# Softmax sums in the middle of a head's turn, and the last head's sums on all partitions

## The chip, the cores and the metric

The kernel runs on one core of a Trainium2 chip. Its time is device microseconds (us) of one launch; the number compared is the median of several runs. The engines are TensorE (PE, matrix products into the eight PSUM banks; its weight loads are listed as PEld), VectorE (DVE), ScalarE (ACT), GpSimd (POOL) and SyncE (SP), whose queue issues nearly all DMA transfers. Each engine works through its own instructions in order and waits on semaphores for the others.

## The reference

Four layers, A, B, A, B, on one sequence of 2048 positions and 640 channels. A is a filter in the frequency domain, and the change doesn't touch it. B is attention in segments of 32 positions with 8 memory positions ahead of each; the memory of a segment is the output of the segment before at those 8 places:

```python
mem = mem0
for s in range(n_seg):                       # 64 segments
    xs = x[:, s * seg_len:(s + 1) * seg_len, :].copy()
    h = jnp.concatenate([mem, xs], axis=1)   # 40 rows
    q, k, v = (einsum('btd,dhe->bhte', h, W) for W in (Wq, Wk, Wv))    # 32 heads of 128
    scores = einsum('bhqe,bhke->bhqk', q, k) * scale
    scores = jnp.where(mask[None, None], scores, -1000000000.0)
    p = _softmax(scores, axis=-1)
    o = einsum('bhqk,bhke->bhqe', p, v)
    o = einsum('bhte,hed->btd', o, Wo)
    mem = o[:, :M, :].copy()
    outs.append(o[:, M:, :])
...
x = x + _A_ref(_layernorm(x), A_w_r, A_w_i)
x = x + _B_ref(_layernorm(x), ...)           # layer 1 below
x = x + _A_ref(_layernorm(x), A_w_r, A_w_i)
x = x + _B_ref(_layernorm(x), ...)           # layer 2 below
```

## The kernel before

**The fast pass.** The kernel guesses the memories, so that all segments can be computed at once, and checks the guess at the end of each B layer; if it fails, or a sum is out of range, a slow exact pass runs (it doesn't run on this input). "Layer 1" and "layer 2" mean the two B layers. Everything here is in `_b_fast_pass`, once per layer. It works on all 64 segments of one head at a time, transposed: the head's 128 features lie on the partitions, the queries (2119 columns: 64 x 32 positions, one memory column a segment and a few more) along the free axis. They form five groups: four of 495 columns (15 segments) and one of 139.

**A head's turn.** The loop over h runs 34 turns for 32 heads, as a pipeline of three stages. Turn h does, in this order:
- for head h, the projections: five key runs (`k_run`, PE L840 into `psk`, copied by DVE L899), five query runs (`q_run`, `psq`, copied by ACT L884 to L892) and value tiles for a pair of heads (`v_tiles`, PE L906 into `psv`, ACT L908), five runs in even turns and four in odd ones. They share three PSUM banks, the pool `pj`.
- for head h-1, nine score parts (`score_part`): PE L916 into `pss` (two banks), ACT takes Exp (L919), DVE multiplies by the mask (L920), which gives P, not normalised.
- for head h-2, five value groups (`value_group`): PE L959 into `pso` (two banks), then DVE multiplies by the inverse softmax sums (L963 for the positions, L965 for the memory column), which frees the bank.

`merge` deals the score parts and value groups evenly between the projection runs, so the score parts stand beside the keys and queries, the value groups beside the last query run and the value tiles. The order on PE, ACT and DVE is that of the code; SP's and POOL's instructions are placed by the framework's scheduler.

**The sums.** At the end of turn h, `sums` adds up P of head h-1 on PE (L934, with 32 columns of ones, one group to 32 partitions of bank `psl`, the fifth group into a free corner of the last score bank), and ACT copies the sums to SBUF (L938 to L940). Behind the first score part of the next turn, ACT takes Ln and Exp(-x) of them (L943, L946), which gives the inverses R. They lie on five rows and are needed on all 128 partitions: SP writes them to DRAM (`Rd`, L948, L949) and a third DMA, L950, broadcasts them into Rb (two buffers). POOL adds R and the sums to two running sums for a range check (`accR` L951, `accS` L952).

**Stores.** At the end of a turn, the head's output goes to DRAM (L972, 512 KB). After every fourth head the first 512 positions of these four heads are loaded back (L975) for the output projection, and that load waits for the store.

**The end of a layer.** In turns 32 and 33 there are no projections left. There `begin` starts three pieces of the output projection, each of 28 matmuls (L1112, into `psx`) over the first 28 heads; the rest of the output projection follows later. The last head's sums go the same way as all others, through DRAM. Behind it stands the memory check (`_b_mem_check`, PE L617), whose range test reads `accR` and `accS` on DVE (L641 to L644).

## Time and profile before

| | |
|---|---|
| median of 3 runs (lowest, highest) | 1707.96 us (1707.82, 1707.96) |
| span of the profiled execution | 1706.2 us |
| layer 1: turns of the loop with all three stages / end of the heads | about 180 to 690 us / 701.6 to 732.1 us |
| layer 2: the same | about 1009 to 1531 us / 1537.0 to 1567.3 us |
| PE busy in layer 2's loop (1009 to 1537 us) | 514.0 of 528.0 us |
| POOL busy in it | 92.0 us |

All rows below come from one profiled execution. A row of the timeline reads: start in us, duration in us, engine, line of the kernel, operation, output <- inputs, shape; in square brackets the time that the engine stood idle before it and what ended that wait. SPq marks the moment when SP issues a DMA; the transfer itself lands later. A row with "x5" holds five like instructions in a row. A row of waits reads: engine, its tile and line, <- what it waited for, then total us, number of waits, the longest. A row of windows reads: stretch, its length, then the busy us of PE, PEld, DVE, ACT and POOL (number of instructions in brackets), mean granted PE clock as a share of the full one, share of DMA time, GB/s.

### The profile page before, as it was taken

The page shows a single profiled execution, that of the slowest core. Times are in us where ns is not written, and L with a number is a line of the kernel's source. Part 1 is how long each engine was busy: PE and PEld are TensorE (multiplying, and loading weights), DVE is VectorE, ACT ScalarE, POOL GpSimd, SP SyncE. Part 2 cuts the span into 40 slices and gives each one's busy share as a digit, 9 for nine tenths or more (in the row PEclk, how much of TensorE's full clock was granted, in tenths as well). Part 3 has the DMA queues.
Part 4 walks back from the last instruction along what each step waited for, and adds up shares of the span by engine and source line. Part 5 has one row for each costly group of instructions (what it writes and reads, how often), then busy time and mean ns, then how long its engine had stood idle before and what let it go on. Part 6 is the DMA issues. An engine that isn't in the chain of part 4 may idle for free. (4 is left out here: it accounts for less than half of the span.)

```text
span 1706.2 us, 36149 instructions
## 1 busy us (share of the span) xinstructions
PE 1570.4 (92%) x14202; PEld 1087.9 (64%) x14203; DVE 906.5 (53%) x2308; ACT 844.0 (49%) x2514; POOL 268.7 (16%) x192
## 2 busy tenths in 40 slices
PE   4887999999999999799987889999999999997998
PEld 2565666666666666577755666666666666665776
DVE  5973465565656555543357725556655665654111
ACT  5363566666666666411114636656666666662000
POOL 0520111121212121200015001112111121211000
PEclk9997999999999999999999989999999999999999
DMA  4562134434343434643301803334343344347232
GB/s 150 170 237 80 62 136 138 139 113 145 128 138 125 141 133 140 218 155 93 94 13 55 283 2 121 125 116 152 133 140 125 135 140 138 115 159 229 66 113 67
DMA packets 168180, 220.23 MB, mean 129 GB/s; under 512 B 7416, under 2 KB 141888, under 8 KB 159808
## 3 DMA queue, kind: packets, MB, share of 16 engines
q1 hardware_dynamic: 167392, 215.53, 37.8%
q8 instruction: 113, 1.85, 0.5%
q0 software_dynamic: 608, 2.30, 0.4%
q14 instruction: 67, 0.55, 0.1%
HBM read 172.69 MB, written 45.11 MB: 128 GB/s over the span
## 5 line engine op out<-in xcount | busy, mean ns | idle before, releaser
L920 DVE TENSOR_TENSOR bB_S<-bB_S,maskf 128x269 bf16<-128x269 bf16 (+5 forms) x576 | 273.2, 475 | 229.4 <-ACT bB_S L919 226.3
L840 PEld LDWEIGHTS <-bB_S 128*128 128x128 bf16 x3180 | 262.7, 97 | 206.6 <-issue 20.8
L1112 PE MATMUL psx<-Wo_sb,bB_S 128*128 128x320 bf16 x2048 | 289.9, 301 | 1.1 <-DVE bB_S L963 1.1
L919 ACT ACTIVATE bB_S<-pss 128x269 bf16<-128x269 f32 (+5 forms) x576 | 224.9, 392 | 112.5 <-PE pss L916 65.3
L963 DVE TENSOR_TENSOR bB_S<-pso,bB_S 128x480 bf16<-128x480 f32 (+1 forms) x320 | 186.0, 582 | 159.0 <-PE pso L959 89.5
L908 ACT CAST bB_S<-psv 128x512 bf16<-128x512 f32 (+1 forms) x288 | 161.8, 562 | 185.7 <-PE psv L906 182.0
L1112 PEld LDWEIGHTS <-bB_S 128*128 128x128 bf16 x2048 | 198.6, 98 | 77.0 <-DVE bB_S L963 1.4
L952 POOL TENSOR_TENSOR bB_S<-bB_S,bB_S 128x634 f32<-128x634 f32 x64 | 98.6, 1540 | 933.1 <-ACT bB_S L940 933.1
L899 DVE CAST bB_S<-psk 128x495 bf16<-128x495 f32 (+3 forms) x320 | 188.9, 591 | 91.5 <-PE psk L840 91.2
L884 ACT ACTIVATE bB_S<-psq 128x480 bf16<-128x480 f32 x300 | 154.2, 514 | 76.2 <-PE psq L840 76.2
L916 PEld LDWEIGHTS <-bB_S 128*128 128x128 bf16 x1216 | 111.3, 98 | 103.2 <-issue 2.3
L906 PE MATMUL psv<-bB_S,B2hT_S 128*128 128x256 bf16 x1360 | 172.3, 274 | 0.2 <-DVE bB_S L899 0.2
L906 PE MATMUL psv<-bB_S,B1hT_S 128*128 128x256 bf16 x1360 | 171.0, 272 | 0.2 <-DVE bB_S L899 0.2
L840 PE MATMUL psk<-B1hT_S,bB_S 128*128 128x495 bf16 (+3 forms) x800 | 162.9, 343 | 1.2 <-DVE B1hT_S L1197 1.2
L840 PE MATMUL psk<-B2hT_S,bB_S 128*128 128x495 bf16 (+3 forms) x800 | 162.9, 343 | 1.2 <-DVE B2hT_S L1197 1.2
L916 PE MATMUL pss<-bB_S 128*128 128x132 bf16 (+8 forms) x1216 | 159.9, 216 | 1.8 <-ACT bB_S L919 1.7
L840 PE MATMUL psq<-B2hT_S,bB_S 128*128 128x495 bf16 (+5 forms) x780 | 154.5, 335 | 7.2 <-DVE bB_S L899 7.2
L840 PE MATMUL psq<-B1hT_S,bB_S 128*128 128x495 bf16 (+5 forms) x780 | 154.5, 335 | 6.7 <-DVE bB_S L899 6.7
L959 PE MATMUL pso<-bB_S,bB_S 128*128 128x132 bf16 (+8 forms) x1216 | 121.2, 218 | 30.0 <-DVE oTmf L965 29.8
L906 PEld LDWEIGHTS <-B2hT_S 128*128 128x128 bf16 x1360 | 127.2, 98 | 13.1 <-issue 0.3
L906 PEld LDWEIGHTS <-B1hT_S 128*128 128x128 bf16 x1360 | 126.5, 98 | 12.6 <-issue 0.3
L959 PEld LDWEIGHTS <-bB_S 128*128 128x128 bf16 x1216 | 92.9, 99 | 44.0 <-DVE oTmf L965 36.9
(216 smaller groups left out, 1553.4 us busy)
## 6 DMA issues: line engine op xcount, KB each, us to landing
bB_S<-Rd SPq DMA_DIRECT2D x64, 1059.5 KB
oTx_d<-bB_S SPq DMA_DIRECT2D x60, 512.0 KB
bB_S<-oTx_d SPq DMA_DIRECT2D x56, 512.0 KB
bB_S<-in_B_Wq_dram SPq DMA_DIRECT2D x32, 320.0 KB
bB_S<-in_B_Wk_dram SPq DMA_DIRECT2D x32, 320.0 KB
bB_S<-in_B_Wv_dram SPq DMA_DIRECT2D x32, 320.0 KB
bB_S<-oTx_d SPq DMA_DIRECT2D x14, 384.0 KB
Wo_sb<-in_B_Wo_dram SPq DMA_DIRECT2D x4, 1280.0 KB
```

Source lines behind the costliest of these rows:

```text
L840: nc.tensor.matmul(ps, lhsT=w[:, ch, hh * 128:(hh + 1) * 128], rhs=src[:, ch, lo:hi], start=(ch == 0), stop=(ch == 4))
L884: nc.scalar.mul(out=qv[:, :, 0:SEG], in_=x_view(ps, o, n)[:, :, 1:SW], mul=scale)
L899: nc.vector.tensor_copy(out=KTs[h % 2][:, lo:hi], in_=ps[:, 0:hi - lo])
L906: nc.tensor.matmul(ps[:, i * 256:(i + 1) * 256], lhsT=hT[:, ch, (t + i) * 128:(t + i + 1) * 128], rhs=w["Wv"][:, ch, :], start=(ch == 0), ...
L908: nc.scalar.copy(out=V[:, t:t + n, :].rearrange("p a b -> p (a b)"), in_=ps[:, 0:n * 256])
L916: nc.tensor.matmul(ps[:, off - o0:off - o0 + hi - lo], lhsT=KT[:, t * 128:(t + 1) * 128], rhs=QT[:, lo:hi], start=True, stop=True)
L919: nc.scalar.activation(out=E[:, 0:n], in_=ps[:, 0:n], func=ACTF.Exp)
L920: nc.vector.tensor_tensor(out=P[:, o0:o0 + n], in0=E[:, 0:n], in1=bs.mask[:, o0:o0 + n], op=ALU.mult)
L952: nc.gpsimd.tensor_tensor(out=accS, in0=accS, in1=sums_sb, op=ALU.add)
L959: nc.tensor.matmul(pso[:, lo - q0:hi - q0], lhsT=V[:, t, (h % 2) * 128:(h % 2 + 1) * 128], rhs=P[:, off:off + hi - lo], start=(i == 0), st ...
L963: nc.vector.tensor_tensor(out=oT.rearrange("p (r s j) -> p r s j", r=16, j=2)[:, :, s0:s0 + ns, :], in0=byclass(po), in1=Rb[:, q0:q0 + nx] ...
L1112: self.tc.nc.tensor.matmul(ps[:, 0:320], lhsT=lhs(h, k // 2), rhs=self.g["Wo_sb"][:, h, c0:c0 + 320], start=(h == 0), stop=(h == H - 1))
```

## The change

Four things are changed, all in layer B:

1. The sums, Ln and Exp with the DMAs of the inverses move. In every turn they stand behind the first, second and third value group (`post`): between the value runs of turn h, not at its end and behind the first score part of the next turn.
2. POOL's addition of the sums (`accS`) goes out at Ln, that of the inverses (`accR`) a head later, at the next head's Ln. R has two buffers, since it is read longer.
3. The last head has no trip through DRAM. `sums_wide` adds up its P on PE with 128 columns of ones, so that each partition has the sums, and ACT writes Ln and Exp straight into Rb, group by group, in the order of P's columns (segment by segment, hence the other view in `value_group`). The banks come from `pj`. The narrow sums of that head are still taken, for the range check alone, behind the value groups of the head before.
4. The order of the two last turns is written out by hand; the third `psx` bank comes from `pj`.

```diff
-    R = g["R"][:]
+    Rs = [s4.f32(GQ + NL), g["R"][:]]
...
-        def sums_ln():
-            nc.scalar.activation(out=R, in_=sums_sb, func=ACTF.Ln, bias=g["floor"][:, 0:1])
+        def sums_ln(h):
+            nc.scalar.activation(out=Rs[h % 2], in_=sums_sb, func=ACTF.Ln, bias=g["floor"][:, 0:1])
+            nc.gpsimd.tensor_tensor(out=accS, in0=accS, in1=sums_sb, op=ALU.add)
+            if h:
+                sums_acc(h - 1)
+
+        def sums_acc(h):
+            nc.gpsimd.tensor_tensor(out=accR, in0=accR, in1=Rs[h % 2], op=ALU.add)

         def sums_back(h):
+            R = Rs[h % 2]
             nc.scalar.activation(out=R, in_=R, func=ACTF.Exp, scale=-1.0)
+            if h == H - 1:
+                return
...
-            nc.gpsimd.tensor_tensor(out=accR, in0=accR, in1=R, op=ALU.add)
-            nc.gpsimd.tensor_tensor(out=accS, in0=accS, in1=sums_sb, op=ALU.add)
+
+        def sums_wide(P, Rb, g_):
+            q0, n = st.q0[g_], st.q0[g_ + 1] - st.q0[g_]
+            ps = pj.tile([128, 512], FP32, name="psw", tag="pj")
+            for i, (t, (_, lo, hi, off)) in enumerate(runs[g_]):
+                nc.tensor.matmul(ps[:, lo - q0:hi - q0], lhsT=ones[:], rhs=P[:, off:off + hi - lo], start=(i == 0), stop=(i == len(runs[g_]) - 1),
+                                 skip_group_check=True)
+            nc.scalar.activation(out=Rb[:, q0:q0 + n], in_=ps[:, 0:n], func=ACTF.Ln, bias=g["floor"][:, 0:1])
+            nc.scalar.activation(out=Rb[:, q0:q0 + n], in_=Rb[:, q0:q0 + n], func=ACTF.Exp, scale=-1.0)
...
-            return (pa if i else pj).tile([128, 512], FP32, name="psx", tag="pss" if i else "pj")
+            return (pa if i == 1 else pj).tile([128, 512], FP32, name="psx", tag="pss" if i == 1 else "pj")
...
+                post = [lambda: None] * 3
                 if 1 <= h <= H:
...
-                if 2 <= h <= H:
-                    Rb[h - 2] = Rbs2[h % 2]
-                    parts[1:1] = [lambda: (sums_ln(), sums_back(h - 2))]
+                    post = [lambda: sums(h - 1, P[h - 1], last_ps[h - 1]), lambda: sums_ln(h - 1), lambda: sums_back(h - 1)]
...
                 if h < H:
-                    merge(dense, parts + groups)
-                if h == H:
+                    g1 = groups + [lambda: None] * (NG - len(groups))
+                    merge(dense, parts + [g1[0], post[0], g1[1], post[1], g1[2], post[2], g1[3], g1[4]])
+                elif h == H:
                     merge(begin(), parts)
-                if 1 <= h <= H:
-                    sums(h - 1, P[h - 1], last_ps[h - 1])
-                if h == H:
-                    Rb[h - 1] = Rbs2[(h - 1) % 2]
-                    sums_ln()
-                    sums_back(h - 1)
-                if h == H:
+                    wide = [lambda g_=g_: sums_wide(P[h - 1], Rb[h - 1], g_) for g_ in range(NG)]
+                    b1 = begin()
+                    wide[0]()
+                    wide[1]()
+                    merge(b1[0:3], wide[2:5])
+                    merge(b1[3:], groups)
+                    post[0]()
+                else:
                     merge(begin(), groups)
-                if h > H:
-                    merge(begin(), [])
-                    merge([lambda: None], groups)
+                    sums_ln(H - 1)
+                    sums_back(H - 1)
+                    sums_acc(H - 1)
```

Below are places in the order of instructions of before and of the changed kernel. A row reads line, operation, output <- inputs, shape; names that begin with bB_S are parts of layer B's large SBUF buffers. Line numbers behind the sums differ between the two: Exp of the sums is L946 before and L953 now, the small writes L948 and L949 are L957 and L958, the broadcast L950 is L959, the value multiplications L963 and L965 are L984 and L985, the store L972 is L992, the load L975 is L995, the output matmuls L1112 are L1134.

ACT before, the end of a late odd turn of layer 1 and the start of the next: the sums are copied behind the last value cast, Ln and Exp follow the first score part's Exp (L919).

```order
L908 CAST bB_S_1585<-psv 128x256
L938 COPY bB_S_1587<-psl 128x480
L939 COPY bB_S_1587<-psl 128x15
L938 COPY bB_S_1587<-pss 32x128
L939 COPY bB_S_1587<-pss 32x4
L940 COPY bB_S_1587<-pss 32x7
L919 ACTIVATE bB_S_1587<-pss 128x283
L943 ACTIVATE R<-bB_S_1587,floor 128x634
L946 ACTIVATE R<-R 128x634
```

ACT now, in the second half of the last turn with projections in layer 1: the copies stand ahead of the last query run's copies (L884, L892, L850), Ln behind them and Exp two value casts later.

```order
L938 COPY bB_S_1587<-psl 128x480
L939 COPY bB_S_1587<-psl 128x15
L938 COPY bB_S_1587<-pss 32x128
L939 COPY bB_S_1587<-pss 32x4
L940 COPY bB_S_1587<-pss 32x7
L884 ACTIVATE bB_S_1586<-psq 128x3x32
L892 ACTIVATE bB_S_1586<-psq 128x4
L850 ACTIVATE bB_S_1586<-psq 128x28
L943 ACTIVATE bB_S_1586<-bB_S_1587,floor 128x634
L908 CAST bB_S_1585<-psv 128x512 x2
L953 ACTIVATE bB_S_1586<-bB_S_1586 128x634
```

So the copies, Ln and Exp all stand half a turn earlier, between value casts.

SP before, at the start of a turn of layer 2 behind a fourth head: the store, the first small write, the load that waits for the store, and only then the second small write and the broadcast.

```order
L972 DMA oTx_d<-bB_S_12783 128x2048
L948 DMA Rd<-R 4x495
L975 DMA bB_S_13229<-oTx_d 128x4x512
L949 DMA Rd<-R 1x139
L950 DMA bB_S_13229<-Rd 128x2119
```

SP now, at such a place: both small writes stand ahead of the store, the broadcast directly behind it and the load behind the broadcast.

```order
L957 DMA Rd<-bB_S_12811 4x495
L958 DMA Rd<-bB_S_12811 1x139
L835 DMA bB_S_12813<-in_B_Wv_dram 128x5x256
L992 DMA oTx_d<-bB_S_12813 128x2048
L959 DMA bB_S_13259<-Rd 128x2119
L995 DMA bB_S_13259<-oTx_d 128x4x512
```

The load has changed places with the broadcast, and the writes with the store.

DVE before, at the end of layer 1's heads, the last value groups of the last head and the range test: L641, which reads a running sum of POOL, has two of the head's five value groups ahead of it, and its reduction L642 a third.

```order
L963 TENSOR_TENSOR bB_S_1588<-pso,bB_S_2034 128x16x30
L965 TENSOR_TENSOR oTmf<-pso,bB_S_2034 128x15
L641 TENSOR_SCALAR bB_S_2034<-bB_S_1585 128x634
L963 TENSOR_TENSOR bB_S_1588<-pso,bB_S_2034 128x16x30
L965 TENSOR_TENSOR oTmf<-pso,bB_S_2034 128x15
L642 TENSOR_REDUCE bB_S_2034<-bB_S_2034 128x1
```

DVE now, at the same place:

```order
L984 TENSOR_TENSOR bB_S_1588<-pso,bB_S_1587 128x16x30
L985 TENSOR_TENSOR oTmf<-pso,bB_S_1587 128x15
L641 TENSOR_SCALAR bB_S_2034<-bB_S_1585 128x634
L642 TENSOR_REDUCE bB_S_2034<-bB_S_2034 128x1
L984 TENSOR_TENSOR bB_S_1588<-pso,bB_S_1587 128x16x30
L985 TENSOR_TENSOR oTmf<-pso,bB_S_1587 128x15
L984 TENSOR_TENSOR bB_S_1588<-pso,bB_S_1587 128x16x8
```

The first part of the range test and its reduction now stand together behind the third value group and ahead of the last full one and the short one; the running sum that L641 reads is now completed by additions behind the narrow sums of the last head.

More of the change, by code (lines that the diff above doesn't have):

```diff
@@ L796, in _b_fast_pass @@
     hT, gq, oTm = bs.hT, bs.gq, bs.oTm
-    ones32 = g["ones32"]
+    ones = g["ones"]
     oTx_d = g["oTx_d"]
@@ L933, in sums @@
                     dst = psl[32 * g_:32 * g_ + 32, :] if g_ < 4 else ps4
-                    nc.tensor.matmul(dst[:, lo - st.q0[g_]:hi - st.q0[g_]], lhsT=ones32[:], rhs=P[:, off:off + hi - lo],
+                    nc.tensor.matmul(dst[:, lo - st.q0[g_]:hi - st.q0[g_]], lhsT=ones[:, 0:32], rhs=P[:, off:off + hi - lo],
                                      start=(i == 0), stop=(i == len(runs[g_]) - 1), skip_group_check=True)
@@ L962, in value_group @@
             po, nx = x_view(pso, 0, ns), ns * SEG
-            nc.vector.tensor_tensor(out=oT.rearrange("p (r s j) -> p r s j", r=16, j=2)[:, :, s0:s0 + ns, :], in0=byclass(po),
-                                    in1=Rb[:, q0:q0 + nx].rearrange("p (r s j) -> p r s j", r=16, j=2), op=ALU.mult)
-            nc.vector.tensor_tensor(out=oTm[:, h, PRE + s0:PRE + s0 + ns], in0=po[:, :, SEG], in1=Rb[:, q0 + nx:q0 + nx + ns], op=ALU.mult)
+            if h < H - 1:
+                rx, rm = Rb[:, q0:q0 + nx].rearrange("p (r s j) -> p r s j", r=16, j=2), Rb[:, q0 + nx:q0 + nx + ns]
+            else:
+                rq = x_view(Rb, q0, ns)
+                rx, rm = byclass(rq), rq[:, :, SEG]
+            nc.vector.tensor_tensor(out=oT.rearrange("p (r s j) -> p r s j", r=16, j=2)[:, :, s0:s0 + ns, :], in0=byclass(po), in1=rx, op=ALU.mult)
+            nc.vector.tensor_tensor(out=oTm[:, h, PRE + s0:PRE + s0 + ns], in0=po[:, :, SEG], in1=rm, op=ALU.mult)
             if g_ < NG - 1:
@@ L1025, in _b_fast_pass @@
                     dense += vt[5:] if h % 2 else vt[:5]
+                post = [lambda: None] * 3
                 if 1 <= h <= H:
                     P[h - 1] = Ps[(h - 1) % 2]
+                    Rb[h - 1] = Rbs2[(h - 1) % 2]
                     parts = [lambda part=part: last_ps.update({h - 1: score_part(h - 1, P[h - 1], part)}) for part in st.parts]
-                if 2 <= h <= H:
-                    Rb[h - 2] = Rbs2[h % 2]
-                    parts[1:1] = [lambda: (sums_ln(), sums_back(h - 2))]
+                    post = [lambda: sums(h - 1, P[h - 1], last_ps[h - 1]), lambda: sums_ln(h - 1), lambda: sums_back(h - 1)]
                 if h >= 2:
@@ L1274, in make_globals @@
     g["Wo_sb"] = sp.tile([128, H, D], BF16, name="Wo_sb")
-    g["ones32"] = sp.tile([128, 32], BF16, name="ones32")
-    nc.vector.memset(g["ones32"][:], 1.0)
+    g["ones"] = sp.tile([128, 128], BF16, name="ones")
+    nc.vector.memset(g["ones"][:], 1.0)
     g["st"] = st = _Stream()
```

1 line of the change is left out of this document (added).

## The prediction

> **What bounds the kernel now.** I read first the page's busy line, then what TensorE (PE) waits for in each layer's head loop, then the timeline of single turns and of the stretch in which a layer's heads end.
>
> ```profile
> PE 1570.4 (92%) x14202; PEld 1087.9 (64%) x14203; DVE 906.5 (53%) x2308; ACT 844.0 (49%) x2514; POOL 268.7 (16%) x192
> ```
>
> PE is the bound and the change takes no work from it: only PE's idle time can be won. PE's waits, layer 1's loop (180 to 690 us) first, then layer 2's (1009 to 1531), as total, times and longest:
>
> ```profile
> PE pso L959 <- DVE oTmf L965: 8.7, 8, 2.1
> PE psq L840 <- DVE bB_S L899: 6.2, 13, 0.5
> ...
> PE psq L840 <- DVE bB_S L899: 7.2, 15, 0.5
> PE pso L959 <- DVE oTmf L965: 6.4, 7, 2.4
> ```
>
> Two waits return: A, 28 times, the first query run waits for a key copy on VectorE (DVE); B, 15 times, a value group waits for DVE to free its bank. A's place in an even turn, where it is absent, and in an odd one:
>
> ```profile
> 1272.60 0.28 PE L916 MATMUL pss<-bB_S 128*128 128x141 bf16 x2
> 1272.72 1.22 PE L840 MATMUL psq<-B2hT_S,bB_S 128*128 128x502 bf16 x5
> ...
> 1286.09 0.68 DVE L899 CAST bB_S<-psk 128x502 bf16<-128x502 f32 x1 [1.19 <-PE psk L840]
> ...
> 1288.26 1.52 POOL L951 TENSOR_TENSOR bB_S<-bB_S,R 128x634 f32<-128x634 f32 x1 [0.69 <-ACT R L946]
> ...
> 1288.43 1.50 DVE L920 TENSOR_TENSOR bB_S<-bB_S,maskf 128x267 bf16<-128x267 bf16 x1
> ...
> 1289.81 0.28 PE L916 MATMUL pss<-bB_S 128*128 128x132 bf16 x2
> ...
> 1290.57 1.22 PE L840 MATMUL psq<-B2hT_S,bB_S 128*128 128x502 bf16 x5 [0.48 <-DVE bB_S L899]
> ...
> 1291.63 0.28 DVE L920 TENSOR_TENSOR bB_S<-bB_S,maskf 128x269 bf16<-128x269 bf16 x1
> ```
>
> The mask multiplication L920 takes 0.28 us with GpSimd (POOL) idle and 1.50 us beside a POOL addition, so DVE copies the keys late. The query run starts 0.12 us after the score part in the even turn and 0.76 us after it in the odd one: **A costs 0.64 us a time**. B is a DMA that lands late:
>
> ```profile
> 1300.93 0.47 SPq L972 DMA_DIRECT2D oTx_d<-bB_S  x1
> ...
> 1306.22 0.36 SPq L975 DMA_DIRECT2D bB_S<-oTx_d  x1
> ...
> 1309.61 0.34 SPq L950 DMA_DIRECT2D bB_S<-Rd  x1
> ...
> 1315.23 0.66 DVE L963 TENSOR_TENSOR bB_S<-pso,bB_S 128x480 bf16<-128x480 f32 x1 [2.85 <-DMA bB_S<-Rd]
> ...
> 1317.60 1.25 PE L906 MATMUL psv<-bB_S,B2hT_S 128*128 128x256 bf16 x10
> ```
>
> Every fourth head the queue stands at L975 until the head's store has landed (5.3 us); the inverses go out behind it, and their broadcast L950 takes 5.6 us. The longest such wait also slows the clock: the ten matmuls behind it take 2.34 us, not 1.25.
>
> ```profile
> 1112.77 0.62 PE L959 MATMUL pso<-bB_S,bB_S 128*128 128x132 bf16 x4 [2.42 <-DVE oTmf L965]
> 1113.18 2.34 PE L906 MATMUL psv<-bB_S,B2hT_S 128*128 128x256 bf16 x10
> ```
>
> Where a layer's heads end, nothing covers that round trip (the two layers' stretches as windows, with PE's busy time second; then rows of layer 2):
>
> ```profile
> 1537.00:1567.30 30.30, 22.07 (x233) 15.76 (x231) 13.56 (x37) 7.69 (x23) 6.14 (x4) 0.89 0.79 262
> 701.60:732.10 30.50, 21.12 (x233) 15.29 (x232) 13.50 (x37) 7.69 (x23) 6.13 (x4) 0.89 0.78 263
> ...
> 1537.01 0.72 PE L1112 MATMUL psx<-Wo_sb,bB_S 128*128 128x320 bf16 x4
> ...
> 1554.32 0.66 DVE L963 TENSOR_TENSOR bB_S<-pso,bB_S 128x480 bf16<-128x480 f32 x1 [9.69 <-DMA Rd<-R]
> ...
> 1555.12 0.62 PE L959 MATMUL pso<-bB_S,bB_S 128*128 128x132 bf16 x4 [6.57 <-DVE oTmf L965]
> 1555.53 2.34 PE L1112 MATMUL psx<-Wo_sb,bB_S 128*128 128x320 bf16 x8
> ```
>
> PE is idle 8.2 and 9.4 us there, and eight matmuls that take 2 x 0.72 us before the wait take 2.34 us after it.
>
> **The change, part by part.** The sum is made against the profiled span, 1706.2 us; the median of the runs is 1707.96 us, so I add 1.8 us at the end.
>
> *Ln, Exp and POOL's sums out of the key stretch.* A POOL pair (1.5 us each) now runs beside the value groups, and the score parts and keys find DVE alone: L920 at 0.28 us and L899 at 0.68 us need 0.96 us of a 1.2 us key run, so A goes: 28 x 0.64 = **17.9 us**. The value multiplications L984 meet POOL instead, which no row shows. The nearest rows are L899, also read from PSUM, 0.68 us while POOL runs (1286.03 to 1287.6), so nothing; and L920, five times as long. At the first price nothing changes; at the second five groups would take 3.3 us each and stall PE. I take the first, since the source is the same, and keep the second for the range. ACT gets five copies, Ln and Exp in the value stretch:
>
> ```profile
> 1285.00 0.56 ACT L938 COPY bB_S<-psl 128x480 f32<-128x480 f32 x1
> ...
> 1285.73 0.16 ACT L940 COPY bB_S<-pss 32x7 f32<-32x7 f32 x1
> ...
> 1313.56 0.58 ACT L908 CAST bB_S<-psv 128x512 bf16<-128x512 f32 x1 [0.75 <-PE psv L906]
> L943 ACT ACTIVATE R<-bB_S,floor 128x634 f32<-128x634 f32 x64 | 52.2, 816 | 0.3 <-DMA Rd<-R 0.2
> L946 ACT ACTIVATE R<-R 128x634 f32<-128x634 f32 x64 | 46.9, 732 | 2.0
> ```
>
> That is 0.9 + 0.8 + 0.7 = 2.4 us, against 0.75 us idle at each of four or five value runs, and three banks let ACT fall behind by a run: hidden. The narrow sums wait for the last score part, but a value group and a query run (1.4 us) stand between. Without that cover they would stall PE by up to a microsecond; only the second turn of a layer has none, since it has no value groups: 1 us a layer, an estimate, **2 us** lost.
>
> *The inverses go out half a turn earlier.* First keys, a weight load, the broadcast and the first value group of an odd turn:
>
> ```profile
> 1284.82 1.23 PE L840 MATMUL psk<-B2hT_S,bB_S 128*128 128x502 bf16 x5
> ...
> 1290.00 0.38 SPq L835 DMA_DIRECT2D bB_S<-in_B_Wk_dram  x1
> ...
> 1290.49 0.46 SPq L950 DMA_DIRECT2D bB_S<-Rd  x1
> ...
> 1295.48 0.41 PE L959 MATMUL pso<-bB_S,bB_S 128*128 128x132 bf16 x4
> ...
> 1296.46 0.66 DVE L963 TENSOR_TENSOR bB_S<-pso,bB_S 128x480 bf16<-128x480 f32 x1
> ```
>
> The group stands 10.7 us into its turn, and 8.6 us without A and the two query runs that now follow it (1.4 us). PE needs the bank back only at the third group, 3.3 us later, so the broadcast may land 11 us into an odd turn (12 us into an even one, which has a value run more). Exp ends about 1 us before the turn does, so the small writes go out there, and the broadcast can start 1 to 2 us into the next turn: landed at 7 to 8 us by the 5.6 us above, with 3 us to spare. But the queue now has the head's store directly ahead of it. The store goes out some 0.4 us into the turn (an estimate: the narrow sums no longer end the turn). If store and broadcast run one after the other, the broadcast lands at 0.4 + 5.3 + 5.6 = 11.3 us, 0.3 us late in odd turns, some 9 us over 30 of them. The oT0 load L975 moves behind the broadcast, and nothing urgent is behind it then. I take the first value, because here the broadcast went out 0.5 us behind a weight load and DVE used it 6.0 us later without a wait; so B goes with its clock loss (1.1 us for the ten matmuls above): 8.7 + 6.4 + 1.1 = **16.2 us**.
>
> [...]
>
> *The last head.* PE's idle 8.2 + 9.4 us and the two clock losses (2.34 against 1.44 us; layer 1's window has the same mean clock, 0.89, so 0.9 us each) go: 19.4 us. Added on PE per layer: five wide sums, priced as the value groups, which read the same columns,
>
> ```profile
> 1563.94 0.64 PE L959 MATMUL pso<-bB_S,bB_S 128*128 128x132 bf16 x8
> 1564.42 0.23 PE L617 MATMUL psm<-oTmf,Wo_sb 128*128 128x71 bf16 x2
> ```
>
> two groups in 0.48 us, so 1.1 us. Their Ln and Exp (495 of 634 columns: 0.64 + 0.57 = 1.2 us) hold two banks, while PE brings four output matmuls and a group (0.8 us) per bank: 3 x 0.4 = 1.2 us of waiting. And a new wait: DVE's check of the ranges, L641, now stands ahead of the last head's fourth value group and waits for three POOL additions (4.6 us) behind the narrow sums' copies (1.1 us); with the check (1.3 us) and two value groups (1.5 us) the last columns are ready 8.5 us after the narrow sums. PE has 28 output matmuls (3.9 us), the groups (1.1 us) and 1.2 us of memory check to do meanwhile: a wait of 2.3 us, about as long as the one that slowed the clock above, so 1 us more. Per layer 1.1 + 1.2 + 3.3 = 5.6 us, both 11.2 us; the end gains 19.4 - 11.2 = **8.2 us**. The bounds are no wait at L641 (15 us) and twice these waits (0 us).
>
> [...]
>
> **Sum**: 17.9 - 2 + 16.2 + 8.2 = 40.3 us. 1706.2 - 40.3 = 1665.9 us of span, **1667.7 us** as timed; I say 1667.
>
> **The rivals.** (1) *The store ahead of the broadcast makes a new wait B*: one after the other, as above, 9 us less, 1677 us. For it: the queue's order. Against it: the weight load of 1290.00, which did not hold its broadcast up. Chance 0.17. (2) *The end trades one wait for another*: L641 and the wide sums cost what the round trip did, 1675 us, 0.12. (3) *Slower*: the broadcast is late in every turn. Its slowest row in a loop, from issue to DVE's start:
>
> ```profile
> 282.97 1.08 SPq L950 DMA_DIRECT2D bB_S<-Rd  x1
> ...
> 290.95 0.66 DVE L963 TENSOR_TENSOR bB_S<-pso,bB_S 128x480 bf16<-128x480 f32 x1 [1.97 <-DMA bB_S<-Rd]
> ```
>
> 8 us behind the whole store land at 13.7 us: 2.7 us late in odd, 1.7 us in even turns, 60 turns, 132 us lost, 1668 + 132 = 1800 us. It turns slower than before from an average of 0.7 us of lateness per turn (40 us over 60 turns), so from 12.2 us on. Against it: so slow a one came beside two weight loads, which now go out later. Chance 0.06. (4) *The change doesn't do what it says*: POOL's pair, beside the value groups, slows DVE there by L920's price and A comes back as another wait, 1667 + 18 = 1685 us, 0.08.
>
> **How the numbers follow.** The forecast has 0.57 (1658 to 1674). The range goes up to (4) and down to what is left if neither the end's new waits nor the second turn's cost anything, 1667 - 11 - 2 and some microseconds for what idle PE costs beyond its records: **1648 to 1686 us**. About 0.2% of the time, 3.4 us, is what a measurement here can tell from no change. The forecast, (1), (2) and (4) hold 0.94, (3) 0.06; of each 0.01 falls within the 0.2%: faster 0.93, slower 0.05, the same 0.02.
>
> **What would show it.** A: L920 at 0.3 us throughout, no wait of psq for L899, odd turns 0.64 us shorter. B: no DVE wait for the broadcast long enough to reach a wait of PE for pso. The end: no wait of 6 us; a wait of PE of 2 to 3 us behind DVE's L641; PE's waits for psw's banks under 1.5 us. I am wrong if the broadcast lands later than 11 us into the turns, if the value multiplications grow beside POOL, or if ACT's Ln and Exp hold back value casts so that psv waits.

## The result, and the profile after

The changed kernel takes **1671.18 us** (median of 4 runs, 1665.58 to 1671.64) against 1707.96 us for the kernel before (four runs, 1707.82 to 1711.95): ratio **0.977, 95% interval 0.975 to 0.980**. The forecast was 1667 us, the range 1648 to 1686 us. The profiled run has a span of 1669.1 us, 37.1 us under that of before. PE's busy time is 1564.6 us, 6 us less, so most of the gain is idle time, as it had to be:

```profile
PE 1564.6 (94%) x14240; PEld 1081.5 (65%) x14241; DVE 810.9 (49%) x2308; ACT 837.0 (50%) x2534; POOL 268.5 (16%) x192
```

Four windows split each span at the first key run of a layer's loop and at the first output matmul of turn 32: loop of layer 1, its end with the layer A that follows, loop of layer 2, its end. The columns are those of the windows above. First the kernel before:

```profile
172.24:701.61 529.37, 513.28 (x4678) 347.50 (x4679) 305.09 (x773) 331.98 (x1027) 91.90 (x60) 1.00 0.38 129
701.61:1008.56 306.95, 267.07 (x2426) 194.05 (x2424) 153.70 (x406) 89.42 (x242) 41.55 (x32) 0.94 0.37 117
1008.56:1537.01 528.45, 514.42 (x4678) 348.88 (x4679) 306.32 (x773) 331.96 (x1027) 91.95 (x60) 1.00 0.38 130
1537.01:1706.20 169.19, 154.62 (x1273) 111.05 (x1271) 31.82 (x88) 9.63 (x33) 6.14 (x4) 0.97 0.38 118
```

Then the changed kernel:

```profile
172.22:687.28 515.06, 512.33 (x4678) 345.54 (x4679) 258.04 (x769) 324.82 (x1033) 93.79 (x62) 1.00 0.39 133
687.28:988.72 301.44, 266.06 (x2446) 193.52 (x2444) 153.43 (x409) 93.02 (x246) 39.60 (x31) 0.96 0.36 117
988.72:1505.63 516.91, 512.32 (x4678) 345.40 (x4679) 258.35 (x769) 324.72 (x1033) 93.75 (x62) 1.00 0.39 132
1505.63:1669.10 163.47, 152.73 (x1294) 110.67 (x1291) 31.41 (x91) 13.31 (x37) 4.19 (x3) 0.99 0.37 117
```

The loops win 14.3 + 11.5 = 25.8 us, the ends 5.5 + 5.7 = 11.2 us. The waits A and B are gone from PE's list in both loops. Here are all of PE's waits in 1009 to 1531 us, a stretch that takes in the first 25 us of layer 2's end. The wait for the key copy L899 belongs to the loop, all others to the end:

```profile
PE psk L840 <- DVE bB_S L899: 2.5, 2, 2.1
PE psx L1134 <- DMA bB_S<-oTx_d: 1.3, 1, 1.3
PE psm L617 <- DVE oTmf L988: 1.0, 1, 1.0
PE psw L965 <- ACT bB_S L967: 0.5, 2, 0.3
PE pc L627 <- DMA bB_S<-oTx_d: 0.3, 1, 0.3
PE pc L627 <- ACT bB_S L625: 0.2, 1, 0.2
```

The group of mask multiplications answers to wait A. Their mean was 475 ns; now it is 287 ns, with none beside POOL:

```profile
L920 DVE TENSOR_TENSOR bB_S<-bB_S,maskf 128x269 bf16<-128x269 bf16 (+5 forms) x576 | 163.1, 287 | 152.6 <-ACT bB_S L919 148.8
```

Odd turns take 15.71 us (16.09 before), even ones still 17.09. One odd turn of before took 15.45 us, so 0.26 us of it is a new loss. The timeline of an odd turn shows where:

```profile
1262.64 0.44 PE L840 MATMUL psk<-B2hT_S,bB_S 128*128 128x128 bf16 x5
1262.92 0.65 PE L916 MATMUL pss<-bB_S 128*128 128x141 bf16 x4
1263.41 1.22 PE L840 MATMUL psq<-B2hT_S,bB_S 128*128 128x502 bf16 x5
```

`merge` deals 17 pieces over 14 runs there, so that two score parts (four matmuls) follow the short key run back to back. They take 0.49 us until the query run starts; elsewhere two such parts take 0.24 us.

### The profile page after: what moved, and what is told of

The parts are those of the page before. It is cut to its first block, busy times and chain, and to the rows that moved or that the text cites. A ratio compares the mean times of both kernels' runs of the same rounds, so it can differ in the third digit from the quotient of the medians.

```text
span 1669.1 us, 36193 instructions
## 1 busy us (share of the span) xinstructions
PE 1564.6 (94%) x14240; PEld 1081.5 (65%) x14241; DVE 810.9 (49%) x2308; ACT 837.0 (50%) x2534; POOL 268.5 (16%) x192
## 5 line engine op out<-in xcount | busy, mean ns | idle before, releaser
L840 PEld LDWEIGHTS <-bB_S 128*128 128x128 bf16 x3180 | 260.3, 97 | 187.1 <-issue 7.8
L984 DVE TENSOR_TENSOR bB_S<-pso,bB_S 128x480 bf16<-128x480 f32 (+1 forms) x320 | 189.5, 593 | 264.7 <-PE pso L975 249.1
L919 ACT ACTIVATE bB_S<-pss 128x269 bf16<-128x269 f32 (+5 forms) x576 | 213.3, 385 | 192.6 <-PE pss L916 177.8
L1134 PE MATMUL psx<-Wo_sb,bB_S 128*128 128x320 bf16 x2048 | 288.2, 299 | 2.9 <-DMA bB_S<-oTx_d 2.9
L1134 PEld LDWEIGHTS <-bB_S 128*128 128x128 bf16 x2048 | 197.2, 98 | 79.5 <-DMA bB_S<-oTx_d 3.6
L899 DVE CAST bB_S<-psk 128x495 bf16<-128x495 f32 (+3 forms) x320 | 191.4, 599 | 115.9 <-PE psk L840 85.6
L920 DVE TENSOR_TENSOR bB_S<-bB_S,maskf 128x269 bf16<-128x269 bf16 (+5 forms) x576 | 163.1, 287 | 152.6 <-ACT bB_S L919 148.8
L884 ACT ACTIVATE bB_S<-psq 128x480 bf16<-128x480 f32 x300 | 152.6, 509 | 98.2 <-PE psq L840 98.2
L840 PE MATMUL psk<-B2hT_S,bB_S 128*128 128x495 bf16 (+3 forms) x800 | 165.0, 342 | 3.7 <-DVE bB_S L899 2.5
L840 PE MATMUL psk<-B1hT_S,bB_S 128*128 128x495 bf16 (+3 forms) x800 | 165.0, 342 | 1.8 <-DVE B1hT_S L1219 1.2
L906 PE MATMUL psv<-bB_S,B2hT_S 128*128 128x256 bf16 x1360 | 163.4, 272 | 0.2 <-DVE bB_S L899 0.2
L906 PE MATMUL psv<-bB_S,B1hT_S 128*128 128x256 bf16 x1360 | 163.4, 272 | 0.2 <-DVE bB_S L899 0.2
L916 PEld LDWEIGHTS <-bB_S 128*128 128x128 bf16 x1216 | 103.0, 98 | 90.1 <-issue 6.4
L916 PE MATMUL pss<-bB_S 128*128 128x132 bf16 (+8 forms) x1216 | 148.3, 216 | 3.1
L975 PE MATMUL pso<-bB_S,bB_S 128*128 128x132 bf16 (+8 forms) x1216 | 119.6, 216 | 0.0
L975 PEld LDWEIGHTS <-bB_S 128*128 128x128 bf16 x1216 | 91.2, 98 | 15.7 <-DVE oTmf L985 0.5
## 6 DMA issues: line engine op xcount, KB each, us to landing
bB_S<-Rd SPq DMA_DIRECT2D x62, 1059.5 KB
```

What stands on the lines that cost most here:

```text
L840: nc.tensor.matmul(ps, lhsT=w[:, ch, hh * 128:(hh + 1) * 128], rhs=src[:, ch, lo:hi], start=(ch == 0), stop=(ch == 4))
L884: nc.scalar.mul(out=qv[:, :, 0:SEG], in_=x_view(ps, o, n)[:, :, 1:SW], mul=scale)
L899: nc.vector.tensor_copy(out=KTs[h % 2][:, lo:hi], in_=ps[:, 0:hi - lo])
L906: nc.tensor.matmul(ps[:, i * 256:(i + 1) * 256], lhsT=hT[:, ch, (t + i) * 128:(t + i + 1) * 128], rhs=w["Wv"][:, ch, :], start=(ch == 0), ...
L916: nc.tensor.matmul(ps[:, off - o0:off - o0 + hi - lo], lhsT=KT[:, t * 128:(t + 1) * 128], rhs=QT[:, lo:hi], start=True, stop=True)
L919: nc.scalar.activation(out=E[:, 0:n], in_=ps[:, 0:n], func=ACTF.Exp)
```

## The experiments

Kernels named b_ start from the kernel before, those named a_ from the changed one. Times are set against the kernel before run on the same chip beside them (1709.5, 1710.4 and 1709.6 us in the three sets).

**b_nopool: POOL's sums left out (wait A alone).** The running sums of the range check are not computed.

```diff
-            nc.gpsimd.tensor_tensor(out=accR, in0=accR, in1=R, op=ALU.add)
-            nc.gpsimd.tensor_tensor(out=accS, in0=accS, in1=sums_sb, op=ALU.add)
```

> The kernel before without GpSimd's two running sums per head (the range check then reads zeros). Theory: the mask multiplication L920 takes 1.50 us instead of 0.28 us only because GpSimd adds beside it, and this alone makes wait A. Then L920 takes about 0.3 us everywhere, the first query run no longer waits for the key copy L899, odd turns fall from 16.09 to 15.45 us, and 28 x 0.64 = 17.9 us go: about 1690 us. Rival: what delays the keys in an odd turn is Ln and Exp on ScalarE, which stand between the score parts' Exps; they stay where they are here. Then the query run goes on waiting, odd turns stay at 16.09 us and the time stays within 0.2% of 1708 us.

Measured: 1700.65 us, ratio 0.994 (0.992 to 0.996). L920 took 288 ns on average, no query run waited, undisturbed odd turns took 15.45 us: the rival (Ln and Exp on ACT) falls. But only 9 us were won, because the other wait grew. PE's waits for pso in the whole kernel, before and in b_nopool:

```profile
PE pso L959 <- DVE oTmf L965: 29.8, 19, 7.7
PE pso L957 <- DVE oTmf L963: 40.2, 25, 8.8
```

**b_load: the load issued by POOL (wait B alone).**

```diff
-                    nc.sync.dma_start(out=oT0[:, a:h + 1, :], in_=oTx_d[:, a:h + 1, 0:512])
+                    nc.gpsimd.dma_start(out=oT0[:, a:h + 1, :], in_=oTx_d[:, a:h + 1, 0:512])
```

> The kernel before with one edit: the load of four heads' first 512 positions (L975) is issued by GpSimd's queue, so that SyncE's queue never stands waiting for the store ahead of the broadcast of the inverses. Theory: wait B is only that place in the queue. Then the waits of value groups L959 for L965 in both loops (8.7 + 6.4 us) and the slowed matmuls behind the longest go, 16.2 us: about 1692 us, and turns of 17.2 to 21.3 us are no longer seen. Rival: the broadcast is late because store, broadcast and load share the DMA engines, whoever issues them; then the waits stay and the time is 1705 to 1709 us.

Measured: 1693.47 us, 0.992 (0.990 to 0.994). The profiled span is 1690.1 us, 16.1 us less, and the long turns went but for three that are 0.7 to 1.2 us too long. The place in SyncE's queue made B. The loops alone are 17.0 us shorter; the two ends together are 1.5 us longer. Wait A stayed (29 times).

**b_both: both edits together.**

> The kernel before, without GpSimd's running sums (the range check reads zeros) and with the load of four heads' positions issued by GpSimd: both causes away, nothing moved. Apart they gave 8.9 and 15.8 us of span-like time (1700.6 and 1690.1 us against 1706.2); in the first, odd turns were 15.45 us, but waits for the broadcast grew from 30 to 40 us. Theory: in shorter turns the broadcast, still issued 8 us into the turn, lands too late for the value groups, so the two do not add up: loops of 515 to 519 us, 1682 to 1688 us. Rival: the growth in the first came from the queue's stand behind the store alone; then odd turns are 15.45 and even turns 17.09 us, loops of 509 to 511 us, and the time is 1672 to 1676 us.

Measured: 1687.32 us, 0.986 (0.984 to 0.989); loops 519.1 and 516.4 us. The two edits together won 22.3 us, near the sum of what they won one by one (8.8 and 16.0 us), but not the 34.1 us that the prediction has for A and B: with both taken away where they stood, value groups still waited for the broadcast (PE 6.4 and 5.3 us in the loops). Shorter turns need the inverses earlier. The change gives that by moving the sums: in its loops PE waits for no value bank, and with new waits of their own they are together 3.6 us shorter than these (515.1 and 516.9 us).

**b_tail: the new end of a layer with the old loop.** The wide sums, the order of the last turns and the third output bank as in the change:

```diff
+                    wide = [lambda g_=g_: sums_wide(P[h - 1], Rb[h - 1], g_) for g_ in range(NG)]
...
+                    merge(b1[0:3], wide[2:5])
+                    merge(b1[3:], groups)
+                    sums(h - 1, P[h - 1], last_ps[h - 1])
```

> The kernel before with only the end of a layer changed: the last head's sums on all partitions by PE, the order of the two last turns and the third output bank as in the change; the loop stays. From the start of turn 32 on the changed kernel is 5.5 and 5.7 us shorter than before in the two layers. Theory: that gain is the end's own, so it appears here too: 11 us, about 1697 us. Rival: half of it needs the inverses of head 30 to come early, which only the changed loop gives; here that head's value groups wait for their broadcast in front of the last head's, and the gain is 4 to 7 us, 1701 to 1704 us.

Measured: 1715.46 us, **slower** by half a percent: 1.005 (1.003 to 1.007). Both theories were wrong; the ends are 308.5 and 172.5 us, 1.5 and 3.3 us longer than before. The long wait stands where it stood:

```profile
1556.88 0.66 DVE L981 TENSOR_TENSOR bB_S<-pso,bB_S 128x480 bf16<-128x480 f32 x1 [11.26 <-DMA bB2x_S<-x]
...
1557.67 0.62 PE L972 MATMUL pso<-bB_S,bB_S 128*128 128x132 bf16 x4 [4.19 <-DVE oTmf L982]
```

These are the first value multiplication and the third value group of head **30**, the last head but one. The first row names the DMA whose semaphore came last by the profile, a load of x; the multiplication also needs head 30's broadcast, which went out only at 1548.42 us.

**a_loop: the new loop with the old end.** Inverses of the last head through DRAM, its sums right behind its score parts.

```diff
-                    wide = [lambda g_=g_: sums_wide(P[h - 1], Rb[h - 1], g_) for g_ in range(NG)]
...
+                    for f in post:
+                        f()
+                    merge(begin(), groups)
```

> The changed kernel with the old end of a layer: the last head's inverses go through DRAM as before, its sums, Ln and Exp directly behind its score parts, the third output bank as before; the loop is that of the change. b_tail, the new end with the old loop, made the kernel 0.5% slower. Theory: the loops keep their 14.3 and 11.5 us, and the old end costs what it cost before or less (306.9 and 169.2 us), so the span is 1680 us, and the two halves of the change add up to more together than apart, as the new end needs head 30's inverses early. Rival: the old end also gains from the early inverses of head 30 (its value groups no longer wait), and the loop alone makes nearly all of the change: 1670 to 1674 us.

Measured: 1668.05 us, 0.976 (0.974 to 0.979), the whole of the change. Its ends:

```profile
686.47:984.80 298.33, 263.77 (x2427) 192.52 (x2425) 151.80 (x409) 87.79 (x236) 39.59 (x31) 0.96 0.38 121
...
1499.43:1664.40 164.97, 153.22 (x1275) 110.86 (x1272) 30.21 (x91) 7.97 (x27) 4.16 (x3) 0.98 0.39 122
```

298.3 + 165.0 = 463.3 us, against 464.9 us for the change: the last head's sums on PE show no gain. They cost VectorE time, too: the four long value multiplications of the last head, which read Rb segment by segment, take 0.95 to 0.99 us each in the changed kernel, those of all other heads 0.66 us. What remains of the wait is again head 30's, and shorter:

```profile
1503.03 0.33 SPq L957 DMA_DIRECT2D bB_S<-Rd  x1
...
1510.98 0.66 DVE L982 TENSOR_TENSOR bB_S<-pso,bB_S 128x480 bf16<-128x480 f32 x1 [5.96 <-DMA bB_S<-Rd]
...
1511.78 0.62 PE L973 MATMUL pso<-bB_S,bB_S 128*128 128x132 bf16 x4 [2.98 <-DVE oTmf L983]
1512.19 2.34 PE L1127 MATMUL psx<-Wo_sb,bB_S 128*128 128x320 bf16 x8
```

**a_deal: another deal in odd turns**, so that the score parts stand as in even turns.

```diff
-                while n * len(dense) < (i + 1) * len(dep):
+                while n < len(dep) and n * max(nd, len(dense)) < (i + 1) * len(dep):
...
-                    merge(dense, parts + [g1[0], post[0], g1[1], post[1], g1[2], post[2], g1[3], g1[4]])
+                    merge(dense, parts + [g1[0], post[0], g1[1], post[1], g1[2], post[2], g1[3], g1[4]], NG + NG + 5 if h >= 2 else 0)
```

> The changed kernel with another deal in odd turns: the 17 pieces (score parts, value groups, sums) are dealt over the 14 projection runs as if there were 15, as in even turns, so that two score parts no longer stand back to back behind the short key run. In the changed kernel odd turns take 15.71 us where the kernel before had one of 15.45 us, and the two parts there take 0.49 us instead of 0.24 us. Theory: the second of them waits for a score bank; with the new deal odd turns fall to about 15.46 us, 30 turns x 0.25 = 7.5 us: about 1663.5 us. Rival: the 0.25 us is another limit of the odd turn, for instance ScalarE's five Exps in the short stretch, and moves to another place: 1669 to 1672 us.

Measured: 1684.99 us, worse than the change. Odd turns are 15.45 us as expected, but even turns rose to some 17.5 us and the ends by 4.7 and 6.4 us. At the ends, PE waits 8.7 us for the last load, where the changed kernel waits 2.9 us. For the even turns, DVE's waits tell why:

```profile
DVE bB_S L899 <- DMA Rd<-bB_S: 66.0, 28, 7.6
```

Here the copy of an even turn's first keys waits for the write of the inverses to DRAM:

```profile
1215.19 0.51 SPq L957 DMA_DIRECT2D Rd<-bB_S  x1
...
1217.55 0.33 SPq L959 DMA_DIRECT2D bB_S<-Rd  x1
1217.65 0.68 DVE L899 CAST bB_S<-psk 128x502 bf16<-128x502 f32 x1 [1.85 <-DMA Rd<-bB_S]
```

The two touch different columns. But the change put R of even heads (`Rs[0]`) into the buffer that holds the keys, and the program has a semaphore wait of the key copy for that write in every even turn but the first. In the changed kernel the write usually lands in time; in turns 2 and 30 it does not (4 waits, 22.2 us of DVE).

**a_rows: the inverses of even heads written row by row**, with which the program has no such wait.

```diff
+            if h % 2:
                 nc.sync.dma_start(out=Rd[0:1, 0:4 * GQ].rearrange("o (g n) -> (o g) n", g=4), in_=R[0:128:32, 0:GQ])
+            else:
+                for q in range(4):
+                    nc.sync.dma_start(out=Rd[0:1, q * GQ:(q + 1) * GQ], in_=R[32 * q:32 * q + 1, 0:GQ])
```

> The changed kernel, where the inverses of even heads, which lie in the buffer of the keys and queries, go to DRAM row by row (four writes of one row each) instead of one write of four rows 32 partitions apart. Theory: VectorE's first key copy of an even turn waits for that strided write to land although it touches other columns; this is the only new wait of the loop, it makes turn 2 (0.8 and 0.7 us longer) and turn 30 (0.6 and 2.5 us longer). Without it no key copy waits for a write of the inverses, turn 2 is 17.1 us, turn 30 is 17.1 us, and 4 to 5 us go against the changed kernel's 1669.1 us of span: 1664 to 1665 us. Rival: turns 2 and 30 are long because the queue is late with the writes (Exp late in turn 2, block loads ahead in turn 30), and three more issues make the broadcast later: the spans stay at 1668 to 1672 us, and value groups begin to wait for the broadcast.

Measured: 1670.72 us, 0.977 (0.975 to 0.980), no different from the change. In the trace the theory holds: turns 2 and 30 are 17.09 us, both loops 513.68 us, 4.6 us less together. But the span did not fall: the ends are 0.7 and 1.4 us longer (the last load is waited for longer, 2.0 and 1.7 us), and the first loop started at 174.2 us instead of 172.2, which the profiles of a_rows_deal, a_order, b_both and a_probe2 (173.5 to 174.3 us) show too and which lies ahead of all that was edited.

**a_rows_deal: both together.**

> The changed kernel with the writes row by row and the deal of a_deal together. a_deal alone brought odd turns to 15.45 us as expected, but its even turns rose from 17.09 to some 17.5 us, and 28 key copies waited for the write of the inverses, 66 us in all, since the sums of odd turns come later there. Theory: that wait is all that was given back. Without it odd turns are 15.45 and even turns 17.09 us, both loops together some 12 us shorter than the changed kernel's (30 x 0.26 + 4.6 us), 1000.56 us from first to last key run becoming 988 to 989 us. The end may keep a_deal's longer wait for the last load (4.2 and 4.5 us). Rival: even turns are long because PE's work of the odd turn spills into them; then they stay at 17.4 to 17.6 us.

Measured: 1670.71 us, 0.977 (0.975 to 0.979). All turns from the third on are 17.09 and 15.45 us, each loop 509.88 us: 12.2 us less, as expected. The ends gave back 9.8 us; PE waits 4.0 us in layer 2's for the last load, which is issued behind the last broadcasts.

**a_order: head 30 ahead of heads 28 and 29 in the rest of the first output sums.**

```diff
-        for h in range(h0, h1):
+        hs = [H - 2, H - 4, H - 3, H - 1] if h0 == H - 4 else range(h0, h1)
+        for h in hs:
```

> The changed kernel with another order of heads in the rest of the first output sums: head 30 (still in SBUF) ahead of heads 28 and 29, which come back from DRAM by the last load. In the changed kernel one output matmul of head 28 stands on PE ahead of the third value group of head 30 and waits 1.6 and 1.3 us for that load. Theory: that wait goes and nothing else is late behind it: 2 to 3 us less. Rival: behind it stands DVE's work on the two last heads, which PE waits for anyway before the memory check, so the time stays within 0.1% of the changed kernel's.

Measured: 1668.76 us, 0.976 (0.973 to 0.978): not told apart from the change by time. The wait for the load went (1.6 and 1.3 us), and two of 1.2 us for head 30's value multiplications came in its place; the ends are 1.3 and 0.1 us shorter.

**a_probe and a_probe2: when does the broadcast land?** A POOL copy of one column of Rb per turn; in the second kernel the store goes out on POOL's queue.

```diff
+                        nc.gpsimd.tensor_copy(out=g["probe"][:], in_=Rb[h - 2][:, 0:1])
```

> The changed kernel, with one GpSimd copy of one column of the broadcast inverses ahead of each turn's score parts: it starts when the broadcast has landed, and so shows the landing, which no row of the changed kernel shows. The broadcast goes out 0.94 us into odd and 1.52 us into even turns, directly behind the store of 512 KB. Theory of the prediction's forecast: both move side by side, and the broadcast lands 5.6 us after its issue, 6.5 to 7.5 us into the turn. Rival: one after the other, the store's 4.3 us and then 5.6 us, so that it lands 10 to 11.5 us into the turn, just ahead of the value groups. The time stays that of the changed kernel within 0.2%.

> The kernel of a_probe with the head's store issued by GpSimd's queue, some 1 us later than SyncE issued it. With the store directly ahead on the same queue the broadcast landed 7.1 to 8.0 us into odd turns (issued at 0.94) and 8.8 to 10.6 us into even ones (issued at 1.52, a weight load and the store ahead). Theory: what is ahead on the queue delays the broadcast by its transfer; without the store it lands 1 to 2 us earlier, about 6 us into odd and 8 us into even turns. Rival: the engines are shared whoever issues, and the landing stays within 0.5 us or comes later.

Measured in a_probe, an odd turn (from 1256.5 us on):

```profile
1257.05 0.32 SPq L992 DMA_DIRECT2D oTx_d<-bB_S  x1
1257.48 0.37 SPq L959 DMA_DIRECT2D bB_S<-Rd  x1
...
1263.72 0.18 POOL L1055 COPY probe<-bB_S 128x1 f32<-128x1 f32 x1 [6.63 <-DMA bB_S<-Rd]
```

The even turn that follows starts at 1272.24 us; its broadcast is issued 1.58 us in and lands here:

```profile
1282.56 0.18 POOL L1055 COPY probe<-bB_S 128x1 f32<-128x1 f32 x1 [9.22 <-DMA bB_S<-Rd]
```

Over both loops it landed 7.1 to 8.0 us into odd and 8.8 to 10.6 us into even turns, ahead of the 11 and 12 us from which it would count: a margin of some 3 and 1.4 us. With the store on another queue it landed 7.7 to 8.4 us and mostly 8.4 to 10.8 us into them, not earlier. So the place behind the store in the queue does not set it, and the rival of a_probe2 holds. The store went out there only 0.3 us later in odd and 0.15 us later in even turns, still just ahead of the broadcast, so what the store's bytes cost the broadcast is not shown. Each of the two kernels ran once: 1668.06 us, and 1677.72 us with the store on POOL's queue.

**a_best: the three repairs together**, with turn 31 and head 30 left as in the change (`2 <= h < H - 1` in the deal, `if h % 2 or h == H - 2` in the writes).

> The changed kernel with the three repairs together: writes row by row for even heads but the last of them (head 30), the deal of a_deal in turns 2 to 30, and head 30 ahead of heads 28 and 29 in the rest of the first output sums. a_rows_deal shortened both loops by 12.2 us, but its end was 9.8 us longer, since the last sums, and with them the last load, came later. Theory: with turn 31 and head 30 left as in the changed kernel and the output order of a_order, the loops keep 12 us (each 510.1 us) and the ends stay at 300.1 and 163.4 us: span some 1656 to 1658 us, about 0.7% under the changed kernel. Rival: the end loses again what the loops win, because its transfers start at the same distance from the loop's end whatever PE does: 1667 to 1671 us.

Measured: **1660.59 us** (1657.43 to 1662.64), ratio to the kernel before 0.971 (0.969 to 0.974), below the change's interval. All four windows as expected:

```profile
171.70:681.85 510.15, 509.49 (x4679) 344.68 (x4680) 260.06 (x769) 323.23 (x1033) 94.05 (x62) 1.00 0.40 134
681.85:981.48 299.63, 265.35 (x2447) 193.55 (x2445) 153.43 (x409) 93.24 (x246) 39.60 (x31) 0.96 0.37 117
981.48:1491.63 510.15, 509.49 (x4679) 344.66 (x4679) 260.07 (x769) 323.24 (x1033) 94.03 (x62) 1.00 0.40 134
1491.63:1655.30 163.67, 152.74 (x1294) 110.59 (x1291) 31.62 (x91) 13.31 (x37) 4.19 (x3) 0.99 0.37 117
```

By these records PE is idle 0.7 us in each loop of 510 us: what could still be won there is work.

## Why the prediction came out right, and where it did not

The total was right to 4 us, and part of that is luck, since the errors cancel: of 37.1 us of span the loops gave 25.8 where 32.1 was said, the ends 11.2 where 8.2 was said.

- **A (17.9 us).** The mechanism is shown by b_nopool: POOL beside the mask multiplication and nothing else. Of 0.64 us an odd turn, 0.38 came in; the other 0.26 us (7.8 us over 30 turns) went into a wait that the prediction didn't see, the two score parts back to back. a_deal shows that this placing was its cause.
- **POOL beside the value multiplications** at no price: right. The long multiplications L984 have a median of 658 ns beside POOL and without it; L963 had 657. (The group's mean rose from 582 to 593 ns mostly by the last head's, which read Rb in another order.) The text on the change says that POOL adds the inverses a head later; in the trace it adds them directly behind the same head's Exp, as the scheduler placed it (row L949 at 1273.11 us, below).
- **B (16.2 us).** Mechanism right (b_load: 16.1 us). As terms of one sum A and B were too simple: b_both has 22.3 of their 34.1 us, and the rest comes only if the inverses come earlier. Where nothing else disturbs (a_best), the loops are 37.5 us shorter than before, so that A and B with their smaller waits were worth more than the 34 us of the sum.
- **The broadcast behind the store.** In odd turns the first value, side by side, holds: landed 7.1 to 8.0 us into the turn where 7 to 8 was said. In even turns it does not: 8.8 to 10.6 us, mostly some 8.3 us after the issue instead of 5.6. That no group waited there is the margin of 12 us, not the forecast's timing. Rival (1), one after the other, 11.3 us in odd turns, falls, and with it rival (3). What rival (1) took for the price of the store, 5.3 us, is the time until a waiter sees it landed; added to the broadcast's 5.6 us it gives 10.9 us from the store's issue, where 6.7 us was measured. That the store ahead costs the broadcast its whole time was the prediction's own estimate. With the store on another queue nothing was won, so no run here shows a cost of the place.
- **The second turn (2 us lost).** It was the third turn, 0.7 to 0.8 us, with 0.2 us in the second, and 0.6 and 2.5 us in turn 30: 5.0 us. 4.6 us of it is the key copy's wait for the write of the inverses, which a_rows takes away, and a step that the prediction lacks: it counted the move of R into another buffer at nothing. The uncovered sums of the second turn cost the other 0.4 us, not 2.
- **The last head (8.2 us).** The size came near (11.2 us), but the step is **wrong**. The prediction took PE's idle 8.2 and 9.4 us for the last head's round trip. The long wait in each, 6.6 and 7.7 us, was head 30's. In the kernel before, the value groups at 1545.44 and 1546.23 us are its first two; the third, at 1555.12 us, is the one that waits. The last head's five only begin at 1563.94 us, and VectorE waits for PE there, not for a broadcast:

```profile
1543.65 0.33 SPq L949 DMA_DIRECT2D Rd<-R  x1
...
1545.44 0.41 PE L959 MATMUL pso<-bB_S,bB_S 128*128 128x132 bf16 x4
...
1545.59 0.33 SPq L950 DMA_DIRECT2D bB_S<-Rd  x1
...
1546.23 0.40 PE L959 MATMUL pso<-bB_S,bB_S 128*128 128x132 bf16 x4
...
1564.39 0.66 DVE L963 TENSOR_TENSOR bB_S<-pso,bB_S 128x480 bf16<-128x480 f32 x1 [4.38 <-PE pso L959]
```

Head 30's sums came at the turn's end, and its writes and broadcast went out between store, load and block loads. So the new loop, with the sums in the middle of the turn, is what shortens the end: a_loop has all of the gain without the wide sums, b_tail has them without the move and is slower. (The move of the sums and that of POOL's additions were not tried apart.) Of the costs put on the end, PE's waits for the wide sums' banks are 1.1 us in both layers together (2.4 said). The wait behind L641 is 1.1 us a layer (2.3 said, and 1 for the clock, which stayed at 1.00 from 687 to 720 and from 1506 to 1540 us): two POOL additions stand ahead of L641, not three, and VectorE waits only 0.3 us for them; the last head's longer multiplications add 1.3 us a layer, which the sum lacks. A wait for the last load, 1.6 and 1.3 us, was not foreseen: the prediction had written that behind the broadcast nothing urgent stood.

Rival (2), the end trades one wait for another, is thus true of the wide sums taken by themselves. Rival (4) falls: what came back as another wait was not POOL's contention but the deal.

What stays open: whether the loop of a_best with the old end would be shorter still (not tried), what makes the broadcast land later in even turns, and why some profiles enter the first loop 2 us late.

## What to carry to other kernels

Before a wait is put down to a piece of work, count the instructions at its place: which head, which turn it belongs to; the name of the buffer doesn't say. When two waits lie behind each other in a pipeline, try each removal alone and both together before adding up prices read from waits. A small buffer that is put into a larger one can bring the waits of that larger one with it, as here, where a DMA reads it with a stride over partitions: look for new semaphore waits on the engines that write the neighbours.

## What the runs showed of the hardware

Two places of the changed kernel's timeline: a value multiplication beside POOL, and a key run behind a wait.

```profile
1273.07 0.66 DVE L984 TENSOR_TENSOR bB_S<-pso,bB_S 128x480 bf16<-128x480 f32 x1 [1.68 <-PE pso L975]
1273.11 1.53 POOL L949 TENSOR_TENSOR bB_S<-bB_S,bB_S 128x634 f32<-128x634 f32 x1 [1.71 <-ACT bB_S L953]
...
1476.26 1.21 PE L840 MATMUL psk<-B2hT_S,bB_S 128*128 128x499 bf16 x5 [2.12 <-DVE bB_S L899]
```

- A DVE multiplication of two SBUF operands (L920) took 1.50 us beside a POOL addition and 0.28 us alone; one with a PSUM operand (L984) took 0.66 us beside POOL, no more than the 0.66 us that L963 took before without it.
- The broadcast (1059.5 KB in the profile's count), issued 0.43 us behind a store of 512 KB, had landed 6.7 us after the store was issued (a_probe); with the two on different queues it came no earlier (a_probe2: 7.7 to 8.4 us into odd turns, against 7.1 to 8.0).
- Behind a wait of PE of 2.98 us (a_loop) eight output matmuls take 2.34 us, against 1.25 us undisturbed (at 1522.04 us of the changed kernel; the prediction took twice the 0.72 us of four). In the kernel before, ten value matmuls took 2.34 us instead of 1.25 behind a wait of 2.42 us, at a granted clock of 0.50 from 1112.72 to 1116.13 us; after 2.12 us, above, a key run took its usual 1.21 us, and the clock was 1.00 from 1474.10 to 1479.00 us.
- The length of a wait does not decide it alone. In a_probe2 a wait of 3.25 us left the clock at 1.00, in b_nopool one of 2.04 us was followed by 3.4 us at 0.50:

```profile
1480.60 1.22 PE L840 MATMUL psk<-B2hT_S,bB_S 128*128 128x499 bf16 x5 [3.25 <-DVE bB_S L899]
1480.60:1482.00 1.40, 1.40 (x12) 0.83 (x12) 1.40 (x5) 0.70 (x3) 0.00 (x0) 1.00 0.90 236
...
593.10 0.41 PE L957 MATMUL pso<-bB_S,bB_S 128*128 128x132 bf16 x4 [2.04 <-DVE oTmf L963]
594.10:597.50 3.40, 3.40 (x37) 2.46 (x35) 1.40 (x7) 1.08 (x3) 0.00 (x0) 0.50 0.00 0
```

- PE's idle time and the clock at three waits: in the kernel before, PE was idle for 2.37 of the 3.41 us from 1109.31 to 1112.72 us (the wait of 2.42 us) and for all of the 3.41 us from 1549.63 to 1553.04 us (within head 30's wait of 6.57 us), both at a clock of 1.00; it was 0.50 behind them, to 1116.13 and to 1559.87 us. In the changed kernel PE was idle for 1.70 of the 3.41 us from 1474.56 to 1477.97 us (the wait of 2.12 us), and the clock stayed at 1.00. For the waits of 3.25 and 2.04 us these rows do not show what decided.
